# One attention-and-experts kernel on one core: q's and k's transposes as two products of 64 rows each, in one block

## The chip, the core and the metric

The kernel runs on one core of a Trainium2 chip. A core has five engines with queues of their own: TensorE (PE; its weight loads are listed apart as PEld), VectorE (DVE), ScalarE (ACT), GpSimd (POOL) and SyncE (SP), which issues most DMAs. Each works through its own instructions in order and waits on semaphores for the others. The metric is the device time of one execution in microseconds.

## What is computed

The reference has three stages. The first is a linear attention with complex decay over 4 batches, 8 heads, 768 positions and 48 channels; the other two are a gated product and a layer of 8 experts on the 3072 tokens that come out of it.

```
for t in range(S):                       # per batch and head
    new_re = ar * S_re - ai * S_im       # a_re, a_im of step t, scaled to a length of at most 0.999
    new_im = ar * S_im + ai * S_re
    kv = outer(k[t], v[t])
    S_re, S_im = new_re + kv, new_im
    y[t] = q[t] @ S_re
x = y as [3072, 384]
x = (x @ w_a * (x @ w_b)) @ w_out        # 384 -> 1536 -> 384
out = x + gate * (relu(x @ w1[e]) @ w2[e])   # for tokens that a score lets through, e their best expert
```

Everything is float32.

## The kernel before

**Attention in units.** The recurrence is done in chunks of 128 positions. A unit is one chunk of one batch with all 8 heads; there are 24, four for each of six chunks, and two units make a pair. For a unit, ACT and DVE work out the running logarithm and the phase of the decay, with cumulative sums on PE ("l", "tp"), and from them the rotated and scaled q and k: tiles "qr" and "kr", 128 positions by 8 heads by 96 numbers (a cosine and a sine part of 48 each).

`att_pe` (from line 389) is a unit's work on PE. It turns each head of qr and kr to 96 x 128, four heads in one PSUM bank ("pq", "pk", lines 422 and 427), and a copy takes each bank to SBUF ("tq", "tk", line 272, on ACT but for three in the first units). From these come the scores k.q. Units 0 to 5 take whole 128 x 128 products ("pc"). Units 6 to 23 take only the part below the diagonal, in strips of 32 columns of the array, into two banks kept for the purpose ("pcs", line 444); DVE masks them ("sc", line 453). "ds" (line 403) is the update of the running state, "y" (line 482) the output: 32 products in strips, half with the state and half with the masked scores. ACT and DVE take y to the tile "xt", and DVE adds ds to the state. Through units 6 to 19 these three groups stand together: 32 products of pcs, 24 of ds, 32 of y; units 20 to 23 have no ds.

PSUM has eight banks: two with the tag "at", which l, tp, pq, pk, ds, y and the routing's small products share in turn, two "at2" (from unit 6 on the two score banks), two "ab" and two "op".

**The gated product runs alongside.** Every pair gives a group of 256 tokens, 12 groups in all. A group has 12 steps of 18 products in split float32 (a high and a low part, so three products for one), "ab" (lines 615 to 617), whose two halves are multiplied on DVE ("asb", line 623) and split again ("gh", "gl"), and 6 products "op" (lines 599 to 601) for the step two back. While PE works on one group's ab and op, the attention of the next pair is threaded between them. Group 6, for example, runs while units 14 and 15 are made. After the last group the experts follow ("eh", "eo").

**What sets the order.** A scheduler places each engine's instructions by its own model of their times, under the kernel's data dependencies. For the first units a list of names in the code (`ORDER`, applied by `keep_rows`) sets the order by hand. Dependencies added by `after(later, earlier, how)` bind further: with `NoSync` they fix the order alone, with `Sync` they are waited for on the chip.

Of the kernel before, what the change touches and what calls it, by code (L numbers as in the profile page):

```python
# [10 lines left out]
F32 = mybir.dt.float32  # L11
# [5 lines left out]
ALU = mybir.AluOpType  # L17
# [62 lines left out]
GF = 5  # L80
WO = DM + 10
# [37 lines left out]
def kern(tc, q, k, v, a_re, a_im, w_a, w_b, w_out, w_skip, w_gate, w1, w2, out):  # L119
# [3 lines left out]
    with st:  # L123
# [213 lines left out]
        def att_trig(i):  # L337
            c, b = units[i]
            d = U[i]
            im = d["im"]  # L340
            t3 = ew.tile([P, W], F32, tag="t3", name=f"t3_{i}")
            t4 = ew.tile([P, W], F32, tag="t4", name=f"t4_{i}")
            tact(out=t4, in_=im, func=AF.Arctan)
            if c > 0:

                cr = ew.tile([1, W], F32, tag="cr", name=f"cr{i}", bufs=1)
                sync.dma_start(cr, carry[b])
                dve.scalar_tensor_tensor(out=t4[:1], in0=cr, scalar=-2.0 * math.pi, in1=t4[:1], op0=ALU.mult, op1=ALU.add)
            tp = at(f"tp_{i}")
            if i < SPL:  # L350
                pe.matmul(tp[:, :W], trit, t4, start=True, stop=True)
            else:
                hi, lo = parts(i, "t", ("t2", "t1"))
                act.activation(out=hi, in_=t4, func=AF.Copy, scale=INV2PI)
                dve.scalar_tensor_tensor(out=lo, in0=t4, scalar=INV2PI, in1=hi, op0=ALU.mult, op1=ALU.subtract)
                cumsum(tp, hi, lo)

            if on("magic", i) is act:
                act.activation(out=t3, in_=tp[:, :W], func=AF.Identity, bias=b_magic)
            else:  # L360
                dve.tensor_scalar(out=t3, in0=tp[:, :W], scalar1=MAGIC, scalar2=None, op0=ALU.add)
            dve.scalar_tensor_tensor(out=t3, in0=t3, scalar=MAGIC, in1=tp[:, :W], op0=ALU.subtract, op1=ALU.subtract)
            if c + 1 < NCH:
                carry[b] = dpool.tile([1, W], F32, name=f"carry{i}")
                sync.dma_start(carry[b], t3[127:128])
            if on("abs", i) is act:
                tact(out=t4, in_=t3, func=AF.Abs)
            else:
                dve.tensor_scalar(out=t4.bitcast(I32), in0=t3.bitcast(I32), scalar1=0x7FFFFFFF, scalar2=None, op0=ALU.bitwise_and)
            tact(out=t4, in_=t4, func=AF.Sin, scale=-TWO_PI_IN, bias=b_hpi)  # L370
            ts = ew.tile([P, W], F32, tag="t1", name=f"ts{i}")
            d["ts"] = ts
            marks["ts", i] = tact(out=ts, in_=t3, func=AF.Sin, scale=-TWO_PI_IN)
            for nm in ("q", "k"):
                tag = "krl" if nm == "k" and i >= 6 and i % 2 else nm + "r"
                r = ew.tile([P, 2 * W], F32, tag=tag, name=f"{nm}r{i}", bufs=1)
                if nm == "k":
                    d["kf"] = r
                r = r.rearrange("t (h x d) -> t h x d", x=2, d=D)
                src = d[nm].rearrange("t (h d) -> t h d", d=D)  # L380
                on(nm + "c", i).tensor_tensor(out=r[:, :, 0], in0=src, in1=t4.rearrange("t (h d) -> t h d", d=D), op=ALU.mult)
                e = on(nm + "s", i)
                ins = e.tensor_tensor(out=r[:, :, 1], in0=src, in1=ts.rearrange("t (h d) -> t h d", d=D), op=ALU.mult)
                if e is dve:
                    mark((nm + "r", i), ins)
                d[nm + "r"] = r
# [3 lines left out]
        def att_pe(i):  # L390
# [3 lines left out]
            sc, qT = [], []  # L394
# [14 lines left out]
            def new_state(ds):  # L409
                s3 = stt.rearrange("p (h e) -> p h e", e=VP)[:, :, :D]  # L410
                d3 = ds[:96, :W].rearrange("p (h e) -> p h e", e=D)
                if c > 0:
                    dve.tensor_tensor(out=s3, in0=s3, in1=d3, op=ALU.add)
                    d3 = s3
# [7 lines left out]
            def turned(hh):  # L422
                pq = at(f"pq{i}_{hh}")
                for j in range(4):
                    pe.transpose(pq[:96, j * P : (j + 1) * P], qr[:, 4 * hh + j].rearrange("t x d -> t (x d)"), ident)  # L425
                tq = ew.tile([96, 512], F32, tag="tq", name=f"tq{i}_{hh}", bufs=2)
                mark(("tq", i, hh), copy(on("tq", 2 * i + hh, act), tq, pq[:96]))
                pk = at(f"pk{i}_{hh}")
                for j in range(4):
                    pe.transpose(pk[:96, j * P : (j + 1) * P], kr[:, 4 * hh + j].rearrange("t x d -> t (x d)"), ident)  # L430
                tk = ew.tile([96, 512], F32, tag="tk", name=f"tk{i}_{hh}", bufs=2)
                done = mark(("tk", i, hh), copy(on("tk", 2 * i + hh, act), tk, pk[:96])).ins
                qT.append(tq)
                return tq, tk, done

            def scores(hh, tq, tk, done, last):
                pc = at(f"pc{i}_{hh}") if i < CAUSAL else env.pc[hh]
                for j in range(4):
                    if i < CAUSAL:
                        last = pe.matmul(pc[:, j * P : (j + 1) * P], tk[:, j * P : (j + 1) * P], tq[:, j * P : (j + 1) * P], start=True, stop=True).ins  # L440
                        continue
                    for x in (0, 1, 2, 3) if j % 2 == 0 else (3, 2, 1, 0):
                        y0, p0 = j * P + STRIP * (x if j % 2 == 0 else 3 - x), STRIP * x
                        ins = pe.matmul(pc[p0 : p0 + STRIP, y0 : (j + 1) * P], tk[:, y0 : y0 + STRIP], tq[:, y0 : (j + 1) * P], start=True, stop=True).ins  # L444
# [13 lines left out]
            halves = []  # L458
            for hh in range(2):
                halves.append(turned(hh))  # L460
                if i < CAUSAL:
                    last, msk = scores(hh, *halves[hh], last)
            if i >= CAUSAL:
                for hh in range(2):
                    last, msk = scores(hh, *halves[hh][:2], halves[1][2], last)
# [12 lines left out]
            for s_, inter, h, col, begin, end in (t for row in zip(*strips) for t in row):  # L478
                p0, hh, j = STRIP * (s_ % 4), h // 4, h % 4
                o = y[p0 : p0 + STRIP, s_ // 4 * P : (s_ // 4 + 1) * P]  # L480
                l, r = (stt, qT[hh][:, j * P : (j + 1) * P]) if inter else (vt, sc[hh][:, j])
# [12 lines left out]
            dve.tensor_tensor(out=xt[:, :, 1, us], in0=y3, in1=xt[:, :, 0, us], op=ALU.subtract)  # L494
# [734 lines left out]
```

## Time and profile before

| | us |
|---|---|
| runs shown: median (lowest to highest) | 845.05 (844.81 to 845.98) |
| the profiled execution: its time | 847.09 |
| its span, from the first to the last instruction | 845.4 |
| PE busy in the span | 799.0 |
| DVE busy | 559.8 |
| ACT busy | 459.7 |
| mean granted clock of PE | 0.997 |

The span is what the trace covers; the profiled execution's time has some 1.7 us around it. A matmul's record lasts from its start until its result is written, and the records of neighbours overlap, so the cost of a product in a stream is the step from one start to the next and not the length of its record. Several equal records in a row are merged to one line with xN. A shape such as `128*96 128x128` is the weights' rows and columns, and the result's rows and columns as they stream. "idle" before an instruction is time in which its engine did nothing, with the engine and line that ended it; "issue" stands where the profile shows nothing that was waited for.

### The profile page before, as it was taken

What the parts mean: (1) busy time and instruction counts of PE and PEld (TensorE: products, weight loads), DVE (VectorE), ACT (ScalarE), POOL (GpSimd) and SP (SyncE); (2) the same over time, 40 slices, a digit from 0 to 9 for tenths busy, and PEclk for the clock granted to TensorE, in tenths of its full rate; (3) what the DMA queues carried; (4) which work ended last, traced back from release to release, by engine and by line L of the source; (5) the groups of instructions that cost most, each with busy time, mean ns of one, the idle gap of its engine ahead of it and who ended that gap; (6) DMA issues with size and microseconds to landing.
All of it is one profiled execution on the core that took longest, in us unless ns stands there. A gap on an engine that the chain in (4) does not pass through costs nothing.

```text
span 845.4 us, 21833 instructions
## 1 busy us (share of the span) xinstructions
PE 799.0 (95%) x8827; PEld 768.4 (91%) x8827; DVE 559.8 (66%) x1339; ACT 459.7 (54%) x949; POOL 235.0 (28%) x274
## 2 busy tenths in 40 slices
PE   1899999999999999999999999999999999999995
PEld 0589899999999999999999999999999989999995
DVE  7899888695884867738677386673736547555541
ACT  6798655364564655636547365473634325555540
POOL 3131353320311113102130031300304125757650
PEclk9999999999999999999999999999999999999998
DMA  9995223152341522313222132111103239776600
GB/s 256 243 299 131 52 58 77 22 126 38 83 90 25 114 53 72 63 26 85 45 72 58 30 84 45 50 38 28 32 2 115 74 118 347 222 223 199 194 22 23
DMA packets 180959, 83.15 MB, mean 98 GB/s; under 512 B 152084, under 2 KB 168026, under 8 KB 180848
## 3 DMA queue, kind: packets, MB, share of 16 engines
q1 hardware_dynamic: 178800, 76.26, 35.2%
q0 software_dynamic: 2048, 5.40, 1.8%
q8 instruction: 71, 1.16, 0.6%
q14 instruction: 40, 0.33, 0.1%
HBM read 69.84 MB, written 12.61 MB: 98 GB/s over the span
## 4 chain that ended last, share of the span: by engine, by line
PE 80%; DVE 10%; issue 4%; ACT 3%; POOL 1%; DMA 1%; POOLq 0%; ACTq 0%; DVEq 0%
PE ab L615 10%; PE ab L616 10%; PE ab L617 10%; PE op L600 5%; PE op L601 5%; PE op L599 5%; PE y L482 4%; PE eh L901 3%; PE eh L902 3%; PE eh L904 3%; PE eo L918 3%; PE eo L919 3%; PE eo L920 3%; PE pcs L444 2%; PE pq L425 2%
## 5 line engine op out<-in xcount | busy, mean ns | idle before, releaser
L615 PE MATMUL ab<-xt,wa 128*128 128x256 f32 x432 | 124.5, 289 | 7.5 <-DVE asb L623 7.3
L615 PE MATMUL ab<-xt,wb 128*128 128x256 f32 x432 | 123.3, 285 | 0.1
L616 PE MATMUL ab<-xt,wb 128*128 128x256 f32 x432 | 122.8, 284 | 0.0
L617 PE MATMUL ab<-xt,wa 128*128 128x256 f32 x432 | 122.5, 284 | 0.0
L616 PE MATMUL ab<-xt,wa 128*128 128x256 f32 x432 | 122.4, 283 | 0.0
L617 PE MATMUL ab<-xt,wb 128*128 128x256 f32 x432 | 122.2, 283 | 0.0
L623 DVE TENSOR_TENSOR asb<-ab,asb 128x256 f32<-128x256 f32 x144 | 60.3, 419 | 73.0 <-ACT asb L272 71.8
L600 PE MATMUL op<-wo,gh 128*128 128x394 f32 x288 | 99.7, 346 | 1.7 <-POOL wo L512 1.7
L601 PE MATMUL op<-wo,gh 128*128 128x394 f32 x288 | 99.6, 346 | 0.0
L599 PE MATMUL op<-wo,gl 128*128 128x394 f32 x288 | 98.6, 346 | 0.0
L272 ACT ACTIVATE asb<-ab 128x256 f32<-128x256 f32 x139 | 53.0, 381 | 70.1 <-PE ab L617 64.1
L615 PEld LDWEIGHTS ab<-xt,wa 128*128 128x128 f32 x432 | 81.3, 189 | 9.9 <-DVE asb L623 9.1
L272 ACT ACTIVATE gh<-asb 128x256 fp32r<-128x256 f32 x132 | 54.7, 415 | 61.2 <-DVE asb L623 61.2
L616 PEld LDWEIGHTS ab<-xt,wb 128*128 128x128 f32 x432 | 81.4, 188 | 1.3 <-issue 1.2
L617 PEld LDWEIGHTS ab<-xt,wb 128*128 128x128 f32 x432 | 81.3, 188 | 1.1 <-issue 1.0
L615 PEld LDWEIGHTS ab<-xt,wb 128*128 128x128 f32 x432 | 81.4, 188 | 0.9 <-issue 0.6
L616 PEld LDWEIGHTS ab<-xt,wa 128*128 128x128 f32 x432 | 81.4, 189 | 0.7 <-issue 0.4
L617 PEld LDWEIGHTS ab<-xt,wa 128*128 128x128 f32 x432 | 81.3, 188 | 0.0
L627 DVE TENSOR_TENSOR gl<-asb,gh 128x256 fp32r<-128x256 f32 x131 | 60.7, 465 | 30.9 <-ACT gh L272 30.2
L869 POOL TENSOR_TENSOR wq<-stg,wq 128x768 fp32r<-128x768 f32 x32 | 59.5, 1862 | 49.1 <-issue 24.8
L320 POOL TENSOR_TENSOR ll<-t,lh 128x384 fp32r<-128x384 f32 x19 | 19.9, 1050 | 163.1 <-ACT lh L272 118.0
L908 DVE SCALAR_TENSOR_TENSOR hl<-eh,hh 128x256 fp32r<-128x256 f32 x64 | 27.1, 424 | 52.2 <-ACT hh L907 52.1
(257 smaller groups left out, 2123.2 us busy)
## 6 DMA issues: line engine op xcount, KB each, us to landing
stg<-in_moe_w_dram SPq DMA_DIRECT2D x28, 768.0 KB
rawa<-in_moe_w_a_dram SPq DMA_DIRECT2D x6, 768.0 KB
re<-in_a_re_dram SPq DMA_DIRECT2D x24, 192.0 KB
rawb<-in_moe_w_b_dram SPq DMA_DIRECT2D x6, 768.0 KB
q<-in_q_dram SPq DMA_DIRECT2D x24, 192.0 KB
k<-in_k_dram SPq DMA_DIRECT2D x24, 192.0 KB
rawo<-in_moe_w_out_dram SPq DMA_DIRECT2D x6, 768.0 KB
xd<-xr SPq DMA_DIRECT2D x24, 192.0 KB
```

The source lines that it names most:

```text
L272: return act.activation(out=out, in_=in_, func=AF.Copy) if e is act else e.tensor_copy(out, in_)
L482: ins = pe.matmul(o, l[:, col : col + STRIP], r, start=begin, stop=end).ins
L599: pe.matmul(o, gl[:, ts], wh, start=f == 0, stop=False)
L600: pe.matmul(o, gh[:, ts], wl, start=False, stop=False)
L601: i = pe.matmul(o, gh[:, ts], wh, start=False, stop=f == NF - 1)
L615: pe.matmul(o, wl, xt[:, c, 0], start=c == 0, stop=False)
L616: pe.matmul(o, wh, xt[:, c, 1], start=False, stop=False)
L617: pe.matmul(o, wh, xt[:, c, 0], start=False, stop=c == NCC - 1)
L623: dve.tensor_tensor(out=asb, in0=ab[:, 256:], in1=asb, op=ALU.mult)
L627: on("gl", n).tensor_tensor(out=gl, in0=asb, in1=gh, op=ALU.subtract)
L869: lo.tensor_tensor(out=o[:, 1], in0=t, in1=o[:, 0], op=ALU.subtract)
L908: vm = dve.scalar_tensor_tensor(out=gl, in0=o, scalar=0.0, in1=gh, op0=ALU.max, op1=ALU.subtract)
```

## The change

For units 6 to 23 `turned` is replaced by `turned_rows`. Instead of one product for a head, which has 128 rows of weights and streams 128 columns of the identity, there are two: positions 64 to 127 and positions 0 to 63, each with 64 rows of weights and 64 columns of the identity. The two halves write two banks, 64 columns of each for each head, so that one bank holds the upper half of all eight heads and the other the lower half. All of q's 16 products come first (into two "at" banks), then all of k's 16 (into the two score banks, before the scores are written there). A chain of `NoSync` dependencies keeps the 32 in this order; the first of them waits for everything that any of them needs. Four copies on ACT follow, two for q and two for k, each writing 8 heads x 64 columns into the one tile "tq" or "tk" of the unit, 96 x 1024, which now have one buffer each instead of two halves with two. Scores and outputs read the same numbers as before from the new places. Units 0 to 5 keep their whole transposes; only their tiles' names change.

```
+ROWS = 64
...
+            tq, tk = (ew.tile([96, H * P], F32, tag=nm, name=f"{nm}{i}", bufs=1) for nm in ("tq", "tk"))
...
-                    pe.transpose(pq[:96, j * P : (j + 1) * P], qr[:, 4 * hh + j].rearrange("t x d -> t (x d)"), ident)
-                tq = ew.tile([96, 512], F32, tag="tq", name=f"tq{i}_{hh}", bufs=2)
-                mark(("tq", i, hh), copy(on("tq", 2 * i + hh, act), tq, pq[:96]))
...
+            def turned_rows(nm, dst, r, banks, last):
+                for h in range(H):
+                    for x, p_ in ((1, banks[1]), (0, banks[0])):
+                        rows = slice(ROWS * x, ROWS * (x + 1))
+                        ins = pe.transpose(p_[:96, h * ROWS : (h + 1) * ROWS], r[rows, h].rearrange("t x d -> t (x d)"), ident[rows, rows]).ins
+                        for w in [last] if last else [d["krw"], marks["t3", i + 1]] if i % 2 == 0 else [d["krw"]] + env.free:
+                            after(ins, w, mybir.DependencyClass.NoSync if last else mybir.DependencyClass.Sync)
+                        last = ins
+                d3 = dst.rearrange("e (h t) -> e h t", t=P)
+                for x, p_ in enumerate(banks):
+                    cp = copy(act if x == 0 else act, d3[:, :, ROWS * x : ROWS * (x + 1)], p_[:96].rearrange("e (h t) -> e h t", t=ROWS))
+                return last, cp.ins
...
-            if i >= CAUSAL:
                 for hh in range(2):
-                    last, msk = scores(hh, *halves[hh][:2], halves[1][2], last)
+                    turned("q", tq, qr, hh)
+                    turned("k", tk, kr, hh)
+                    last, msk = scores(hh, None, last)
+            else:
+                last, _ = turned_rows("q", tq, qr, [at(f"pq{i}_{x}") for x in range(2)], None)
+                _, done = turned_rows("k", tk, kr, env.pc, last)
+                last = None
+                for hh in range(2):
+                    last, msk = scores(hh, done, last)
```

`d["krw"]` is the instruction that writes the second part of kr, `marks["t3", i + 1]` the one that last reads the phase's bank of the pair's other unit, and `env.free` holds the last readers of the previous unit's y and ds banks.

The scheduler then places everything anew. In the orders below a name's first number is the unit (or, for ab, the group and the step), the last a running one.

PE, group 6, around the first transposes of unit 15, before: four of q, five ab products, four of k.

```order
L616 MATMUL ab6_9_6340<-xt6_5085,wa4_1129 128x256
L425 MATMUL pq15_0_5936<-ident_66,qr15_5799 96x128 x4
L617 MATMUL ab6_9_6340<-xt6_5085,wa4_1129 128x256
L615 MATMUL ab6_9_6340<-xt6_5085,wa4_1129 128x256
L616 MATMUL ab6_9_6340<-xt6_5085,wa4_1129 128x256
L617 MATMUL ab6_9_6340<-xt6_5085,wa4_1129 128x256
L615 MATMUL ab6_9_6340<-xt6_5085,wb4_1191 128x256
L430 MATMUL pk15_0_5943<-ident_66,kr15_5802 96x128 x4
```

And in the changed program the start of the same unit's block.

```order
L630 MATMUL ab6_8_6416<-xt6_5157,wb4_1183 128x256
L628 MATMUL ab6_8_6416<-xt6_5157,wb4_1183 128x256
L629 MATMUL ab6_8_6416<-xt6_5157,wb4_1183 128x256
L436 MATMUL pq15_1_6035<-ident_66,qr15_5883 96x64
L436 MATMUL pq15_0_6034<-ident_66,qr15_5883 96x64
L436 MATMUL pq15_1_6035<-ident_66,qr15_5883 96x64
L436 MATMUL pq15_0_6034<-ident_66,qr15_5883 96x64
```

The pieces of four among ab products have become one run of 32 products, which alternate between two banks.

PE, group 6, inside the output y of unit 14, before: y runs on from the products with the first masked half (sc14_0) to the second (sc14_1).

```order
L482 MATMUL y14_5896<-tq14_1_5826,state2_104 32x128 x2
L482 MATMUL y14_5896<-tq14_0_5812,state2_104 32x128
L482 MATMUL y14_5896<-sc14_0_5851,v14_4885 32x128
L482 MATMUL y14_5896<-sc14_1_5869,v14_4885 32x128
L482 MATMUL y14_5896<-tq14_1_5826,state2_104 32x128
L482 MATMUL y14_5896<-sc14_0_5851,v14_4885 32x128
```

And in the changed program at the same place.

```order
L495 MATMUL y14_5992<-tq14_5891,state2_104 32x128 x3
L495 MATMUL y14_5992<-sc14_0_5947,v14_4945 32x128
L628 MATMUL ab6_7_6384<-xt6_5157,wa3_1042 128x256
L629 MATMUL ab6_7_6384<-xt6_5157,wa3_1042 128x256
L630 MATMUL ab6_7_6384<-xt6_5157,wa3_1042 128x256
L628 MATMUL ab6_7_6384<-xt6_5157,wa3_1042 128x256
L629 MATMUL ab6_7_6384<-xt6_5157,wa3_1042 128x256
L630 MATMUL ab6_7_6384<-xt6_5157,wa3_1042 128x256
L628 MATMUL ab6_7_6384<-xt6_5157,wa3_1042 128x256
L495 MATMUL y14_5992<-sc14_1_5965,v14_4945 32x128
```

Seven ab products now stand between y's first 14 products and the other 18.

ACT, the copies of unit 14's transposes, before: they stand among activations for unit 16 (t1, t2) and the copies of group 6.

```order
L272 ACTIVATE tq14_0_5812<-pq14_0_5807 96x512
L223 ACTIVATE t1_16_6459<-t1_16_6459,b_tiny_80 128x384
L272 ACTIVATE asb6_5_6237<-ab6_5_6212 128x256
L272 ACTIVATE tk14_0_5819<-pk14_0_5814 96x512
L223 ACTIVATE t2_16_6460<-t1_16_6459,b_eps_78 128x384
L272 ACTIVATE gh6_5_6240<-asb6_5_6237 128x256
```

And in the changed program.

```order
L273 ACTIVATE tq14_5891<-pq14_1_5894 96x8x64
L273 ACTIVATE tq14_5891<-pq14_0_5893 96x8x64
L224 ACTIVATE t2_16_6568<-t1_16_6567,b_eps_78 128x384
L273 ACTIVATE tk14_5892<-pcs1_2189 96x8x64
L273 ACTIVATE tk14_5892<-pcs0_2188 96x8x64
L273 ACTIVATE asb6_5_6345<-ab6_5_6320 128x256
```

The four copies stand nearly together, and the copy of the ab tile (asb6_5) has moved behind them.

## Rows read from the trace of the kernel before

**Rows 1.** The page, parts 1 and 4: busy time of PE, and the chain.

```profile
PE 799.0 (95%) x8827; PEld 768.4 (91%) x8827; DVE 559.8 (66%) x1339; ACT 459.7 (54%) x949; POOL 235.0 (28%) x274
...
PE 80%; DVE 10%; issue 4%; ACT 3%; POOL 1%; DMA 1%; POOLq 0%; ACTq 0%; DVEq 0%
```

**Rows 2.** Sums by stage: the stretch of units 6 to 23.

```profile
core 0: us, PE busy (x) PEld busy (x) DVE busy (x) ACT busy (x) POOL busy (x), PEclk, DMA share, GB/s
185.00:640.00 455.00, 445.32 (x5764) 431.26 (x5763) 296.54 (x781) 246.56 (x540) 77.28 (x97) 1.00 0.25 54
```

**Rows 3.** Waits of PE in that stretch: total us, times, longest.

```profile
PE ab L615 <- DVE asb L623: 6.6, 7, 1.0
PE y L482 <- issue: 1.9, 3, 0.8
PE y L482 <- DVE sc L453: 0.9, 1, 0.9
```

**Rows 4.** The transposes from 160 to 645 us: count, ns min/median/max, first and last.

```profile
L425 PE MATMUL pq<-ident,qr x144: 270/272/315, 181.0 to 629.5; 128*96 128x128 f32 x144
...
L430 PE MATMUL pk<-ident,kr x144: 270/272/274, 183.6 to 632.9; 128*96 128x128 f32 x144
```

**Rows 5.** Timeline of PE around four transposes: start, length, instruction.

```profile
184.98 0.28 PE L617 MATMUL ab<-xt,wa 128*128 128x256 f32 x1
...
185.21 0.28 PE L616 MATMUL ab<-xt,wa 128*128 128x256 f32 x1
185.34 0.60 PE L425 MATMUL pq<-ident,qr 128*96 128x128 f32 x4
185.69 0.36 PE L617 MATMUL ab<-xt,wa 128*128 128x256 f32 x1
185.89 0.28 PE L615 MATMUL ab<-xt,wa 128*128 128x256 f32 x1
```

**Rows 6.** Timeline of PE: three records of "pc", unit 5.

```profile
150.94 0.50 PE L440 MATMUL pc<-tq,tk 96*128 96x128 f32 x3
```

**Rows 7.** Timeline of PE: unit 22's y, from the ab before.

```profile
622.84 0.28 PE L616 MATMUL ab<-xt,wb 128*128 128x256 f32 x1
623.04 0.43 PE L482 MATMUL y<-tq,state 96*32 96x128 f32 x8
...
624.94 0.64 PE L425 MATMUL pq<-ident,qr 128*96 128x128 f32 x4
...
625.54 0.28 PE L615 MATMUL ab<-xt,wb 128*128 128x256 f32 x1
```

**Rows 8.** Timeline of PE: pcs, ds and y of unit 14, the ab around them.

```profile
408.52 0.28 PE L615 MATMUL ab<-xt,wa 128*128 128x256 f32 x1
...
412.63 0.28 PE L617 MATMUL ab<-xt,wa 128*128 128x256 f32 x1
```

**Rows 9.** The same of unit 12, with one ab within y.

```profile
354.08 0.28 PE L617 MATMUL ab<-xt,wa 128*128 128x256 f32 x1
...
357.09 0.39 PE L615 MATMUL ab<-xt,wb 128*128 128x256 f32 x1
...
358.85 0.28 PE L617 MATMUL ab<-xt,wb 128*128 128x256 f32 x1
```

**Rows 10.** The copies of q's transposes on ACT, 160 to 645 us; tk alike.

```profile
L272 ACT ACTIVATE tq<-pq x36: 574/594/596, 182.5 to 629.9; 96x512 f32<-96x512 f32 x36
```

**Rows 11.** Timeline of weight loads, unit 21: window ending 575.12, then 575.16.

```profile
575.11 0.12 PEld L425 LDWEIGHTS pq<-ident,qr 128*96 128x96 f32 x1 [0.20 <-issue]
...
575.11 0.17 PEld L425 LDWEIGHTS pq<-ident,qr 128*96 128x96 f32 x2 [0.20 <-issue]
```

**Rows 12.** Timeline of PE: six records of "wt".

```profile
45.21 0.84 PE L561 MATMUL wt<-wg,wtt 128*128 128x10 f32 x6 [0.19 <-ACT wtt L272]
```

**Rows 13.** Timeline of weight loads of "ds", unit 6.

```profile
194.39 0.17 PEld L403 LDWEIGHTS ds<-v,kr 128*32 128x32 f32 x6
194.48 0.16 PEld L403 LDWEIGHTS ds<-u,kr 128*32 128x32 f32 x6
```

More of the change, by code (lines that the diff above doesn't have):

```diff
@@ L361, in att_trig @@
                 dve.tensor_scalar(out=t3, in0=tp[:, :W], scalar1=MAGIC, scalar2=None, op0=ALU.add)
-            dve.scalar_tensor_tensor(out=t3, in0=t3, scalar=MAGIC, in1=tp[:, :W], op0=ALU.subtract, op1=ALU.subtract)
+            marks["t3", i] = dve.scalar_tensor_tensor(out=t3, in0=t3, scalar=MAGIC, in1=tp[:, :W], op0=ALU.subtract, op1=ALU.subtract).ins
             if c + 1 < NCH:
@@ L383, in att_trig @@
                 ins = e.tensor_tensor(out=r[:, :, 1], in0=src, in1=ts.rearrange("t (h d) -> t h d", d=D), op=ALU.mult)
+                d[nm + "rw"] = ins.ins
                 if e is dve:
@@ L393, in att_pe @@
             qr, kr, vt, ee = d["qr"], d["kr"], d["v"], d["ee"]
-            sc, qT = [], []
+            sc = []
             stt = state[b]
@@ L412, in new_state @@
                 if c > 0:
-                    dve.tensor_tensor(out=s3, in0=s3, in1=d3, op=ALU.add)
+                    env.free.append(dve.tensor_tensor(out=s3, in0=s3, in1=d3, op=ALU.add).ins)
                     d3 = s3
@@ L420, in att_pe, with turned @@
             last = None
-            def turned(hh):
-                pq = at(f"pq{i}_{hh}")
+            tq, tk = (ew.tile([96, H * P], F32, tag=nm, name=f"{nm}{i}", bufs=1) for nm in ("tq", "tk"))
+            def turned(nm, dst, r, hh):
+                p_ = at(f"p{nm}{i}_{hh}")
                 for j in range(4):
-                    pe.transpose(pq[:96, j * P : (j + 1) * P], qr[:, 4 * hh + j].rearrange("t x d -> t (x d)"), ident)
-                tq = ew.tile([96, 512], F32, tag="tq", name=f"tq{i}_{hh}", bufs=2)
-                mark(("tq", i, hh), copy(on("tq", 2 * i + hh, act), tq, pq[:96]))
[L428 to L434, printed above, removed]
@@ L436, in scores @@
-            def scores(hh, tq, tk, done, last):
+                    pe.transpose(p_[:96, j * P : (j + 1) * P], r[:, 4 * hh + j].rearrange("t x d -> t (x d)"), ident)
+                mark(("t" + nm, i, hh), copy(on("t" + nm, 2 * i + hh, act), dst[:, 4 * P * hh : 4 * P * (hh + 1)], p_[:96]))
+            def turned_rows(nm, dst, r, banks, last):
[10 more added lines that the diff above has]
+                return last, cp.ins
@@ L437, in scores @@
+            def scores(hh, done, last):
                 pc = at(f"pc{i}_{hh}") if i < CAUSAL else env.pc[hh]
                 for j in range(4):
+                    tks, tqs = (x[:, (4 * hh + j) * P : (4 * hh + j + 1) * P] for x in (tk, tq))
                     if i < CAUSAL:
-                        last = pe.matmul(pc[:, j * P : (j + 1) * P], tk[:, j * P : (j + 1) * P], tq[:, j * P : (j + 1) * P], start=True, stop=True).ins
+                        last = pe.matmul(pc[:, j * P : (j + 1) * P], tks, tqs, start=True, stop=True).ins
@@ L441, in scores @@
                         continue
                     for x in (0, 1, 2, 3) if j % 2 == 0 else (3, 2, 1, 0):
-                        y0, p0 = j * P + STRIP * (x if j % 2 == 0 else 3 - x), STRIP * x
-                        ins = pe.matmul(pc[p0 : p0 + STRIP, y0 : (j + 1) * P], tk[:, y0 : y0 + STRIP], tq[:, y0 : (j + 1) * P], start=True, stop=True).ins
+                        y0, p0 = STRIP * (x if j % 2 == 0 else 3 - x), STRIP * x
+                        ins = pe.matmul(pc[p0 : p0 + STRIP, j * P + y0 : (j + 1) * P], tks[:, y0 : y0 + STRIP], tqs[:, y0:], start=True, stop=True).ins
@@ L456, in scores @@
                 return last, msk
[L458 to L462, printed above, removed]
-            if i >= CAUSAL:
-                for hh in range(2):
-                    last, msk = scores(hh, *halves[hh][:2], halves[1][2], last)
+            if i < CAUSAL:
+                for hh in range(2):
+                    turned("q", tq, qr, hh)
[7 more added lines that the diff above has]
+                    last, msk = scores(hh, done, last)
             pcs = last
@@ L480, in att_pe @@
                 o = y[p0 : p0 + STRIP, s_ // 4 * P : (s_ // 4 + 1) * P]
-                l, r = (stt, qT[hh][:, j * P : (j + 1) * P]) if inter else (vt, sc[hh][:, j])
+                l, r = (stt, tq[:, h * P : (h + 1) * P]) if inter else (vt, sc[hh][:, j])
                 ins = pe.matmul(o, l[:, col : col + STRIP], r, start=begin, stop=end).ins
@@ L493, in att_pe @@
             act.activation(out=xt[:, :, 0, us], in_=y3, func=AF.Copy)
-            dve.tensor_tensor(out=xt[:, :, 1, us], in0=y3, in1=xt[:, :, 0, us], op=ALU.subtract)
+            env.free = [dve.tensor_tensor(out=xt[:, :, 1, us], in0=y3, in1=xt[:, :, 0, us], op=ALU.subtract).ins]
             if c + 1 < NCH:
```

4 rows, old and new, of the table ORDER are left out of this document.

## The prediction

> **What bounds the kernel now.** I read the page first. TensorE (PE) is busy for 799.0 of 845.4 us, and it is 80% of the chain that ended last; VectorE (DVE) is 10% [rows 1]. Then the sums by stage: from 185 to 640 us, where units 6 to 23 run, PE is busy for 445.3 of 455.0 us at the full granted clock [rows 2]. What is missing there is told by the view of waits: seven waits of about 1 us at a group's start, where an "ab" product waits for DVE to empty a bank (6.6 us), one wait of 0.9 us of "y" for the mask "sc", and three of 1.9 us in all at "y" that the view puts down to "issue", that is, to nothing it can see [rows 3]. So in this stage a microsecond that PE saves ends the kernel a microsecond sooner, unless a new wait takes it. ScalarE (ACT), which copies the transposed tiles out, is busy for 246.6 of these 455 us [rows 2].
>
> **The transposes as they are.** Each unit has 8 of q and 8 of k: 144 records on each of two lines over 18 units, one record for each [rows 4]. Four of them stand between two ab products, recorded as x4 in 0.60 us where one takes 0.27; so they follow each other every 0.11 us [rows 5]. What four cost is read from the ab products around them: from the last one before (185.21) to the second one after (185.89) is 0.68 us; two steps of an undisturbed ab stream (184.98 to 185.21, 0.12 each) take 0.24. The difference, 0.44, is four times 0.11: nothing is lost in going from ab to a transpose and back. A unit pays 16 x 0.11 = 1.75 us, all on the engine that bounds.
>
> **The new block.** It has 32 products instead of 16, each of half the rows and half the columns. If time goes with columns that stream, one takes 0.055 us; if the two row halves work side by side, the 32 take 16 x 0.055 = 0.88 us. The trace of before has no product of 64 rows, so side-by-side work is judged by the nearest thing: "y" places its products in four strips of 32 columns of the array. A unit's y has 32 products of 128 columns, and each is recorded twice, 64 records; "pc", the same number of columns in the full array, steps every (0.50-0.28)/2 = 0.11 us [rows 6]; 64 of them in a row would take 7.0 us. The y of 623.04 is over, and the next transpose begins, at 624.94: 1.90 us [rows 7]. So four strips do work side by side, and I take two row halves to do the same.
>
> Going in and out of the strips costs something that the transposes now don't pay. In rows 7, from the ab product before (622.84) to the second one after (625.54) is 2.70 us; less 0.24 for two ab steps, 0.44 for the four transposes in between and 64 x 0.11/4 = 1.76 for y leaves 0.26. A second estimate: one unit in before has its y interrupted by a single ab product, another does not. Without interruption, 408.52 to 412.63 less two ab steps is 3.87 us [rows 8]; with it, 354.08 to 358.85 less three steps is 4.41 [rows 9]. One more way out and back is 0.54. For the block I take the middle, 0.40; its ends are 0 (as for the transposes of rows 5) and 0.54.
>
> TensorEngine Tiling in the Trainium skill (Key Properties) says that a change of tiling mode, not merely of the tile, drains the engine; the 0.26 and 0.54 agree for strips, and no run here shows it for halves. Without such a drain the block would save 0.87 a unit instead of 0.47.
>
> So: 0.88 + 0.40 = 1.28 instead of 1.75, a saving of 0.47 us a unit, **8.5 us** over 18 units (ends: with 0.54, 0.33 x 18 = 5.9; with 0, 0.87 x 18 = 15.7).
>
> **What the new order adds.** The order on PE shows y interrupted more often: in before only two units have it; in the changed program seven even units have it, three of them twice, ten in all. Eight more interruptions at 0.54 are **4.3 us** back. Were they cheaper, as 0.26, it would be 2.1. What they could win is the wait that they fill: of the four waits at y (2.8 us, rows 3) the 0.9 for the mask is before y's fifth product, where most of the new pauses don't stand; the other three have no cause shown. A pause gives whatever is late there 1 or 2 us, so I count a third of the 2.8, **0.9 us**, won; the ends are 0 and 2.8.
>
> **What costs nothing, and its cover.** The copies on ACT stay 72 of 0.59 us [rows 10], two for q and two for k, but now back to back. Between the block's end and the scores PE has at least 27 ab and op products, over 3 us; q's copies begin when half the block is done, and all four, with one other activation between them, are done 0.6 + 4 x 0.59 + 0.6 = 3.6 us after the block began, 2.3 after it ended. If ACT ran late by more than 1 us, scores would wait, at 18 places. Four ACT instructions in a row hold back the copy of the ab tile queued behind them; its bank is wanted again only a whole ab tile and six op products later (3.2 us at the earliest, and in most units after the scores), so nothing waits. The block's own added waits (k's rotated tile and the phase of the pair's next unit, or the y and state of the unit before) are for work that DVE now has queued ahead of the ab tile whose turn comes 2 to 3 us before the block; behind a late one stands all of PE. I count none and keep 2 us for it. k now goes to the banks of the scores, last read by the masks of the unit before, over 3 us earlier. The seven waits at group starts stay: DVE has the same routing work before the same tile, in a slightly other order; 1 us either way.
>
> **Sum** against the profiled execution (span 845.4, its time 847.09, the median of the runs 845.05): -8.5 + 4.3 - 0.9 = -5.1 us. The profiled execution is 2.0 above the median and the change is far from its start and end, so I take the same difference from the median: 845.05 - 5.1 = 839.95, **840.0 us**.
>
> **Rivals.** *Loads one after another (slower).* Each product needs its own load of 96 columns. Two loads that found the queue empty ended 0.05 us apart: 0.12 from the start for the first, 0.17 for both [rows 11]; at 0.045 each, 32 in a row take 1.44, and with 0.40 the block takes 1.84, 0.09 more than now. Then +1.6 + 4.3 - 0.9 = +5.0, 850.1 us. The change loses from a block of 1.75 - (4.3 - 0.9)/18 = 1.56 on, a pair of loads of (1.56 - 0.40)/16 = 0.072 us. For it: nothing shows two row halves loading at once. Against it: a load of 128 columns alone sets the pace of "wt", whose products have ten columns: (0.84-0.26)/5 = 0.116 each [rows 12]; by that, 32 columns would take 0.029 one after another, but the strips of "ds" load six in 0.09, that is 0.015 each [rows 13]. So tiles load at least two at a time. Chance 0.17.
>
> TensorE: Matmul & The Clock Gate in the Trainium skill (LDWEIGHTS) gives a load as its columns over 1.2, 80 ns for 96 of them whatever the rows; in a queue of one that would be 2.56 us a block, +21.8 us, 866. Rows 11 show about 50 for this kind, so the page's figure is not used, though its rule that rows don't shorten a load is what this rival lives on.
>
> *The halves don't work side by side at all (slower).* 32 x 0.055 + 0.40 = 2.16, +0.41 a unit, +7.4 + 4.3 - 0.9 = +10.8: 856. Rows 7 speak against it. Chance 0.06.
>
> *No price for the mode, waits filled (much faster).* -15.7 + 2.1 - 2.8 = -16.4: 828.6; half of the way there, 834. Rows 7 to 9 speak against it. Chance 0.12.
>
> *It saves, but the pauses and a new wait eat it.* The block saves 5.9, pauses cost 4.3, nothing is won, 1.6 is lost in waits: 0, 845. Chance 0.10.
>
> The forecast has 0.55, with its own range 836 to 843. The range of 0.8 runs from 832 to 850.5: it leaves out the far ends of the first and the third rival and the whole of the second. This kernel's runs tell a change from none at about 0.2%, 1.7 us: faster 0.68 (the forecast, the third rival and a little of the last), same 0.08, slower 0.24.
>
> **What would show it.** In the changed profile: the step between pairs in the block (0.055 or 0.06 us a pair means side by side; 0.09 loads in a row; 0.11 no gain); the block from the last ab before to the second after, less two steps, near 1.28; the ways out of y at 0.54 each; the waits on PE between 185 and 640 us still near 9 us, none of them at pq, none at pcs. If the step is 0.055 and the time is not below 843, the pauses or a new wait have eaten it and my 4.3 is too small; if pq waits for DVE, the added waits were not free.

## The result, and the profile after

The changed kernel takes 837.55 us (median of four runs, 836.57 to 838.70), beside it the kernel before 845.32 (844.81 to 845.98): a ratio of 0.9906, 95% interval 0.9893 to 0.9918, 7.8 us less. Forecast were 840.0, 5.1 less. The profiled execution has a span of 837.0 us and a time of 838.70, the slowest of the four; against that of before both are 8.4 us less, and what the start and the clock did in these two executions has a part in that (below).

The page of the changed kernel, busy time of the engines, then the sums of the stage of [rows 2] and the waits of PE in it, as in [rows 3].

```profile
PE 791.7 (95%) x9115; PEld 754.5 (90%) x9115; DVE 552.8 (66%) x1339; ACT 455.6 (54%) x949; POOL 234.1 (28%) x274
```

```profile
185.00:640.00 455.00, 447.00 (x6129) 425.35 (x6128) 294.88 (x788) 245.24 (x543) 81.04 (x101) 1.00 0.26 56
```

```profile
PE y L495 <- DVE sc L463: 6.2, 4, 2.4
PE ab L628 <- DVE asb L636: 1.2, 2, 0.8
PE y L495 <- issue: 0.5, 1, 0.5
```

Two things are to be seen. PE is still what bounds: 447 of 455 us. And the waits have changed places: the seven of 1 us at the groups' starts are two, while y now waits 6.2 us for DVE's masks where it waited 0.9.

The timeline of PE around a block, unit 21 (in place of [rows 5]; start, length, instruction).

```profile
570.31 0.28 PE L628 MATMUL ab<-xt,wb 128*128 128x256 f32 x1
570.51 0.65 PE L436 MATMUL pq<-ident,qr 64*96 64x64 f32 x16
571.00 0.61 PE L436 MATMUL pcs<-ident,kr 64*96 64x64 f32 x16
571.54 0.39 PE L629 MATMUL ab<-xt,wb 128*128 128x256 f32 x1
571.77 0.28 PE L630 MATMUL ab<-xt,wb 128*128 128x256 f32 x1
```

From the ab before to the second one after is 1.46 us; less two ab steps, 1.22. Over the 18 units it is 1.22 to 1.24. Inside, by the trace's nanoseconds, the two halves of a head start 3 to 4 ns apart and the next pair 56 ns later: two halves together take 0.056 us where a whole product took 0.11.

Unit 12, whose y now has two pauses, that is, runs of other products inside it (in place of [rows 9]).

```profile
352.13 0.28 PE L630 MATMUL ab<-xt,wa 128*128 128x256 f32 x1
...
354.49 0.39 PE L628 MATMUL ab<-xt,wb 128*128 128x256 f32 x1
...
355.73 0.39 PE L629 MATMUL ab<-xt,wb 128*128 128x256 f32 x1
...
356.54 0.28 PE L629 MATMUL ab<-xt,wb 128*128 128x256 f32 x1
...
358.20 0.34 PE L612 MATMUL op<-wo,gl 128*128 128x394 f32 x1
```

352.13 to 358.20 holds pcs, ds, y and ten ab steps (0.12 each): 6.07 - 1.18 = 4.9 us for what takes 3.9 in one piece. I measured every stretch of pcs, ds and y of units 6 to 23 in this way, less the idle time within: 71.8 us in 24 stretches before, 76.1 in 32 after. Eight more ways out and back cost 4.3 us, 0.54 each, but 0.6 of it is not theirs. From 246.3 to 249.6 us, in and behind unit 8's y, the granted clock of this execution was 0.50, the lower level of 1.2 GHz:

```profile
246.30:249.60 3.30, 3.30 (x28) 2.92 (x26) 2.76 (x6) 1.35 (x3) 1.22 (x1) 0.50 0.33 63
```

```profile
245.98 0.30 PE L495 MATMUL y<-sc,v 128*32 128x128 f32 x1 [1.97 <-DVE sc L463]
...
247.69 0.41 PE L628 MATMUL ab<-xt,wa 128*128 128x256 f32 x1
247.90 0.41 PE L629 MATMUL ab<-xt,wa 128*128 128x256 f32 x1
```

An ab step took 0.21 us there instead of 0.12, and the stretch of unit 8 before its pause 3.8 us instead of the 3.2 of units 6 and 10. Without that the eight cost 3.7 us, 0.46 each. All 3.4 us at half the rate cost some 1.7 us, an estimate. Before the clock fell PE had waited 1.97 us for a mask; in e2_apart it fell behind a wait of 1.98 us (195.0 to 198.4 us at 0.50), in e12_two_blocks within one of 2.3 us (327.0 to 333.8). The wait of 2.42 us in unit 6 had nothing of the kind behind it. So that the waits cost clock as well is possible, and not shown.

DVE around unit 6's masks ("sc"; "chk" is a reload of unit 0's input for a range test, "re" that of a later unit), and PE's y.

```profile
191.41 0.55 DVE L282 TENSOR_REDUCE immax<-chk 128x1 f32<-128x384 f32 x1 [1.26 <-DMA chk<-in_a_im_dram]
...
192.68 0.68 DVE L463 TENSOR_TENSOR sc<-pcs,keep 128x512 int32<-128x512 int32 x1
```

```profile
193.42 0.30 PE L495 MATMUL y<-sc,v 128*32 128x128 f32 x1 [2.42 <-DVE sc L463]
```

DVE stands still for 1.26 us at a test whose reload has not landed; behind the test come two more operations and then the mask. In before the same test ran at 191.59, after a standstill of 0.32, but unit 6's y began only at 195.1 instead of 190.5: the block gave the scores earlier, and they met a queue that had not been cleared for them.

At a group's start, kernel before: the last product of l on PE, the first asb on DVE, the ab product that waits for it.

```profile
271.44 0.34 PE L265 MATMUL l<-lh,tri_r 128*128 128x384 f32 x1
...
278.22 0.39 PE L615 MATMUL ab<-xt,wa 128*128 128x256 f32 x1 [1.00 <-DVE asb L623]
```

```profile
277.75 0.41 DVE L623 TENSOR_TENSOR asb<-ab,asb 128x256 f32<-128x256 f32 x1
```

The same after.

```profile
271.80 0.33 PE L266 MATMUL l<-lh,tri_r 128*128 128x384 f32 x1
...
278.72 0.39 PE L628 MATMUL ab<-xt,wa 128*128 128x256 f32 x1
```

```profile
278.25 0.42 DVE L636 TENSOR_TENSOR asb<-ab,asb 128x256 f32<-128x256 f32 x1
```

From l to asb it is 6.3 us before and 6.45 after: a chain through ACT and DVE that PE cannot shorten. But after, six more op products (step 10 of the group, 1.07 us) stand behind l instead of ahead of it, so PE has work until asb is done.

**The account of the profiled spans:** blocks 18 x (1.75 - 1.23) = -9.4; more pauses +3.7; the stretch at clock 0.50 some +1.7; waits at y (2.8 to 6.7) +3.9; waits at groups' starts (7.3 to 1.2, unit 22's among them) -6.1; a short wait gone, -0.2; the start -1.2; sum -7.6 of -8.4, so that 0.8 is not accounted for. The start is no work of the change: the warming products, the same in both, ran at nearly half the rate in before's profiled execution.

```profile
L583 PE MATMUL warm<-ts,ident x4: 847/847/1006, 25.1 to 27.1; 128*128 128x384 f32 x4
```

```profile
L596 PE MATMUL warm<-ts,ident x4: 486/486/590, 25.0 to 26.1; 128*128 128x384 f32 x4
```

### The profile page after: what moved, and what is told of

Its sections match the earlier page's. It is cut to its first block, busy times and chain, and to the rows that moved or that the text cites. A ratio compares the mean times of both kernels' runs of the same rounds, so it can differ in the third digit from the quotient of the medians.

```text
span 837.0 us, 22417 instructions
## 1 busy us (share of the span) xinstructions
PE 791.7 (95%) x9115; PEld 754.5 (90%) x9115; DVE 552.8 (66%) x1339; ACT 455.6 (54%) x949; POOL 234.1 (28%) x274
## 4 chain that ended last, share of the span: by engine, by line
PE 78%; DVE 7%; ACT 6%; DMA 4%; issue 3%; POOL 1%; SPq 0%; POOLq 0%; ACTq 0%; DVEq 0%
PE ab L628 11%; PE ab L630 10%; PE ab L629 10%; PE op L613 5%; PE op L614 5%; PE op L612 5%; PE y L495 5%; PE eh L914 3%; PE eh L915 3%; PE eh L917 3%; PE eo L931 3%; PE eo L932 3%; PE eo L933 3%; ACT t L224 2%; PE pcs L454 2%
## 5 line engine op out<-in xcount | busy, mean ns | idle before, releaser
L613 PE MATMUL op<-wo,gh 128*128 128x394 f32 x288 | 99.6, 346 | 1.7 <-POOL wo L525 1.7
L614 PE MATMUL op<-wo,gh 128*128 128x394 f32 x288 | 99.2, 344 | 0.0
L612 PE MATMUL op<-wo,gl 128*128 128x394 f32 x288 | 98.8, 346 | 0.0
L640 DVE TENSOR_TENSOR gl<-asb,gh 128x256 fp32r<-128x256 f32 x131 | 58.9, 450 | 30.4 <-ACT gh L273 29.8
```

Of the source, the lines that this page charges most:

```text
L612: pe.matmul(o, gl[:, ts], wh, start=f == 0, stop=False)
L613: pe.matmul(o, gh[:, ts], wl, start=False, stop=False)
L614: i = pe.matmul(o, gh[:, ts], wh, start=False, stop=f == NF - 1)
L640: on("gl", n).tensor_tensor(out=gl, in0=asb, in1=gh, op=ALU.subtract)
```

## The experiments

Ratios are to runs of the kernel before on the same chip (medians there 846.4 to 846.7 us); 0.0012 is 1 us. The changed kernel has 0.9906.

**Whole transposes in the block (e1_whole).** Edit of the changed kernel:

```
-                    for x, p_ in ((1, banks[1]), (0, banks[0])):
-                        rows = slice(ROWS * x, ROWS * (x + 1))
-                        ins = pe.transpose(p_[:96, h * ROWS : (h + 1) * ROWS], r[rows, h]..., ident[rows, rows]).ins
+                    for p_ in (banks[h // 4],):
+                        ins = pe.transpose(p_[:96, h % 4 * P : (h % 4 + 1) * P], r[:, h]..., ident).ins
...
```

The copies change with it: each takes four whole heads of one bank.

> The changed kernel with one part undone: the 16 transposes of a unit are made of whole 128 rows again (16 products instead of 32, head h into bank h // 4, plain 96x512 copies), still all in one block and with the new order of the work around it. Theory (the two halves of a head run side by side, and that is the gain): a unit's block goes from 1.23 us, changes of tile mode included, to 16 x 0.109 = 1.75 us, +0.52 us for each of 18 units, so +9.4 us: 847 us (845.5 to 848.5), 1.011 times the changed kernel. Rival (the gain is the new order of the work, the fewer waits at the groups' starts, and the halves only pay for their own changes of mode): within 2 us of the changed kernel's 837.6 us.

Measured: 845.95 us, ratio 0.9992 (0.9982 to 1.0003), 7.3 us above the changed kernel. The block is 1.75 us in each unit, 9.4 us more in all; PE's waits are 3.0 us fewer (8.0 to 5.0), which gives 6.4; two more pauses (34 stretches, 77.5 us) make up for most of the rest. So the halves carry the gain; the rest of such an order, pauses included, is worth nothing by itself.

**The halves one after another (e2_apart).** The two loops changed places: eight upper halves, then eight lower ones.

> The changed kernel with the halves not alternated: in each block first the eight heads' second halves, then the eight heads' first halves, so that neighbours in the queue use the same 64 rows. Theory (a pair is cheap because its two halves run beside each other): the 32 products take 32 x 0.055 = 1.76 us and with the way in and out 2.1 us instead of 1.23: +0.88 us x 18 = +16 us, 853.5 us (850 to 856). Rival (a half is cheap by itself, since it has half the rows): block and time stay, 837.6 us within 1.5.

Measured: 843.82 us (840.26 to 845.72), ratio 0.9956 (0.9939 to 0.9973): +4.2, neither the theory's number nor the rival's. PE in unit 21's block:

```profile
575.23 0.28 PE L628 MATMUL ab<-xt,wb 128*128 128x256 f32 x1
575.44 0.75 PE L436 MATMUL pq<-ident,qr 64*96 64x64 f32 x13
575.98 0.26 PE L436 MATMUL pcs<-ident,kr 64*96 64x64 f32 x1
576.03 0.22 PE L436 MATMUL pq<-ident,qr 64*96 64x64 f32 x1
...
576.18 0.71 PE L436 MATMUL pcs<-ident,kr 64*96 64x64 f32 x13
576.82 0.39 PE L629 MATMUL ab<-xt,wb 128*128 128x256 f32 x1
577.05 0.28 PE L630 MATMUL ab<-xt,wb 128*128 128x256 f32 x1
```

The block is 577.05 - 575.23 - 0.24 = 1.58 us, 1.59 on the average of the 18. Within one half the products follow each other every 56 ns, as the theory has it: a half alone is not cheap. But at each change of half the next one's products start while the last three or so of the other half are still to start (k's first at 575.98, between q's). At three borders that hides some 9 of 32 steps, 0.5 us. The block costs 0.36 x 18 = 6.6 us more, fewer waits (8.0 to 6.4) give 1.6 back: +5.0, within the interval. In every run of halves the bank changes with the half, so no run tells the rows from the banks; for whole products a change of bank does nothing, as op steps 0.18 us within a bank (L613 to L614) and into the other one (L614 to L612) alike.

**The range tests behind the masks (e3_tests_late).**

```
-                test(i, t)
+                after(test(i, t).ins, marks["sc", i + 6, 1])
```

> The changed kernel with the range tests of units 0 to 5 (the two DVE operations on reloaded inputs that stand in the queue around units 6 to 11) put behind the masks of the unit they used to stand in front of; the same work is done. Theory (y of units 6, 8 and 10 waits 2.4, 2.0 and 1.6 us because DVE stands still at a test whose reload has not landed, with the mask behind it): these waits go but for a few tenths: -5 us, 832.5 us (831 to 834.5). Rival A (the masks are late from DVE's own work, of which the tests are only 0.55 us each): -1 to -2 us, 836. Rival B (the standstill only moves behind the mask, and the next step's asb waits for it): 837 to 838.

Measured: 833.41 us, ratio 0.9839 (0.9826 to 0.9852), -5.7. PE's waits:

```profile
PE ab L628 <- DVE asb L636: 0.8, 2, 0.5
PE y L495 <- issue: 0.6, 2, 0.3
PE y L495 <- DVE sc L463: 0.6, 3, 0.2
```

The 6.2 us are 0.6. The theory stands: DVE's standstill at the reloads made them, not its own work (the tests' 0.55 us each).

**y without pauses (e7_whole_y).** On top of e3_tests_late, with `late` called for ab of steps 7 and 8 and op of steps 5 and 6:

```
+        def late(g, ins, here):
+            if here and 2 <= g <= 8:
+                after(ins, env.yl[2 * g + 2])      # the last product of that unit's y
```

> The kernel e3_tests_late with y of units 6, 8, 10, 12, 14, 16 and 18 made in one piece: the products that stood in its pauses (up to 12) come behind it. The same work is done. Theory (each pause costs the column products' way out and in again: 0.75 us for a unit with one pause, 0.95 with two): seven units give back 5.5 to 6 us, less new waits of y for its masks of up to 0.3 us each, so 828.5 us (827 to 831) where e3_tests_late is 832.5. Rival (the pauses cost nothing, as their products have to be made anyway, and without them y waits for the masks as long as they lasted, 0.8 us and more each): 1 us faster to 5 us slower than e3_tests_late.

Measured: 835.02 us, ratio 0.9858 (0.9844 to 0.9872), 1.6 slower than e3_tests_late. By the intervals that is at the edge of no difference at all, but far from the theory's 5 faster: the rival holds.

```profile
PE y L496 <- DVE sc L464: 4.6, 13, 0.9
PE y L496 <- issue: 1.0, 2, 0.6
```

Seven units lose their pauses and y waits 4.4 us more (5.6 for 1.2). A pause has its price, but here it filled a wait at least as large. What makes the masks late is in DVE's rows of unit 12, kernel e3_tests_late:

```profile
347.87 0.55 DVE L279 TENSOR_SCALAR_CACHE_REDUCE re<-re 128x384 f32<-128x384 f32 x1 [0.24 <-DMA re<-in_a_re_dram]
...
348.35 0.69 DVE L463 TENSOR_TENSOR sc<-pcs,keep 128x512 int32<-128x512 int32 x1
348.95 0.55 DVE L312 SCALAR_TENSOR_TENSOR t<-t,t 128x384 f32<-128x384 f32 x1
349.42 0.68 DVE L463 TENSOR_TENSOR sc<-pcs,keep 128x512 int32<-128x512 int32 x1
```

In the even units the next pair's test, waiting for its own load, and an operation on t stand ahead of and between the masks.

**The masks first (e8_masks_first).** On top of e3_tests_late, for the test `least` and the operation on t1 of unit i:

```
+            if i >= 8:
+                after(ins.ins, marks["sc", i - 2, 1])
```

> The kernel e3_tests_late with the two DVE operations of unit i (8 and up) that stood between or before the masks of unit i - 2 put behind them: the range test of a_re, which waits for its load, and the operation on t before l. The same work is done. Theory (y waits or is paused in the even units because DVE stands at a test whose load has not landed, with a mask behind it; a pause costs the way out and in): y is whole in every unit and takes 3.88 us as in the odd units, instead of 4.63 (one pause) and 4.8 to 5.2 (two): seven units give 0.75 to 1.2 us each, -6 us against e3_tests_late: 827.5 us where that was 833.4 (825.5 to 829.5). Rival (the postponed test makes l, and with it the next unit's transposes, late by what it spared y): 832 to 835.

Measured: 827.92 us, ratio 0.9780 (0.9768 to 0.9793): 5.0 less than e3_tests_late by the ratios, 10.7 less than the changed kernel, 18.6 less than before. The same work is done, and it is the fastest of all. With the masks early the scheduler left y whole in every unit of its own accord. PE at unit 12, then DVE's masks there:

```profile
341.03 0.28 PE L633 MATMUL ab<-xt,wa 128*128 128x256 f32 x1
341.24 1.33 PE L459 MATMUL pcs<-tq,tk 96*32 96x128 f32 x64
...
345.14 0.28 PE L635 MATMUL ab<-xt,wa 128*128 128x256 f32 x1
```

```profile
342.10 1.29 DVE L468 TENSOR_TENSOR sc<-pcs,keep 128x512 int32<-128x512 int32 x2
```

4.11 less two steps is 3.87 us, the number of [rows 8]. All stretches of pcs, ds and y together are 69.7 us in 22, against 76.0 in 33 in e3_tests_late.

**Only the halves undone there (e11_masks_whole).** The edit of e1_whole in e8_masks_first.

> The kernel e8_masks_first with whole transposes of 128 rows in its blocks (16 products, as in e1_whole): only the halves are undone, where neither pauses nor waits at y can answer. Theory (a block costs 1.23 us with alternated halves, 1.75 whole): +0.52 x 18 = +9.4 us against e8_masks_first (8.4 to 10.4). Rival (part of the halves' gain was only fewer waits): +4 to +7 us, as the step from the changed kernel to e1_whole was +7.3.

Measured: 835.40 us, ratio 0.9871 (0.9856 to 0.9886), +7.5 to +7.7, between the theory and the rival. Its blocks are 1.75 us, again 9.4 in all; PE waits 1.0 us less than in e8_masks_first (2.6 to 1.6), the stretches are 0.6 shorter: 7.8. So the theory's 9.4 is the block's price, and what surrounds it took 1.6 to 2 us of it, in a kernel with hardly a wait to give.

**Step 10's op products behind l, in before (e5_before_op).**

```
+                if i >= 8:
+                    for x in env.op:               # the first op products of step 10, one per bank
+                        after(x, marks["l2"])
```

> The kernel before (whole transposes, four apiece among the others) with one thing of the changed kernel's order added: in the groups with units 8 and up, the six op products of the group's step 10 come behind the next units' l products instead of before them. No work is added or taken away. Theory (the fewer waits of ab for asb at the groups' starts are 6.1 us of the changed kernel's 8.4, and come from this place alone: the chain from l by ACT and DVE to asb takes some 6.2 us in either kernel, and 1.07 us more of PE's work stands behind l): the eight waits of 0.92 to 1.0 us go to under 0.2, so -6 us against before: 0.993 of it, 840.3 us where before is 846.4 (839 to 842). Rival (DVE's order of the routing and asb sets them, so they stay or turn up elsewhere): 845 to 847.5.

Measured: 842.57 us, ratio 0.9954 (0.9940 to 0.9967): -3.9, less than the theory's 6 and more than the rival.

```profile
PE y L485 <- DVE sc L456: 2.8, 4, 1.0
PE ab L620 <- DVE asb L628: 0.7, 2, 0.4
```

The cause of the waits is shown: of 7.3 us of waits for asb 1.4 are left in all (0.7 in this stretch, the rest at unit 22's). The time got only 3.9, as the new order gave y two more pauses: the stretches went from 71.8 to 73.3 us, +1.5.

**The masks first in before (e9_before_masks).** Both edits of e8_masks_first in the kernel before.

> The same two edits as e8_masks_first (late tests of units 0 to 5, masks ahead of the next units' test and t) made in the kernel before, which has whole transposes. Theory: before has only 2.8 us of waits at y and two pauses (1.1 us) to give back: -3.5 us, 843 us where before is 846.4 (841 to 845), so that the changed kernel's advantage grows from 8 us to some 15. Rival (the waits are as large in before, hidden under other names, and it gains as much as the changed kernel, 11 us): 835 us.

Measured: 847.99 us, ratio 1.0013 (1.0002 to 1.0025), a miss: 1.1 slower.

```profile
PE pt L755 <- POOL sl L743: 4.5, 5, 1.0
PE ab L620 <- DVE asb L628: 3.0, 3, 1.4
PE ab L621 <- DVE xt L499: 1.5, 4, 0.7
```

Its waits at y are nearly gone (2.8 to 0.8) and no y is paused (71.8 to 70.0). But in its order the second unit's l and the routing stand among the group's first ab products and no longer ahead of them, and PE waits for POOL's and DVE's part of the routing and for xt: 11.1 us of waits in all where there were 10.4. These sums make -1.1, not +1.1; the 2 us between are not accounted for. So the edits that are worth 10.7 us after the change are worth nothing before it; why the scheduler put l there was not tried.

**Two blocks instead of one (e12_two_blocks).** In e8_masks_first k's first transpose waits for the copy of q's.

> The kernel e8_masks_first with a unit's block of 32 half products cut into two blocks of 16, q's and k's, with 11 to 28 full products between them. No work is added. Theory (each way out of full products and in again costs a block 0.35 to 0.40 us: 1.23 us = 32 x 0.027 + 0.36): 18 more of them, +6.5 us against e8_masks_first (5.5 to 8), 834.4 us where that was 827.9. Rival (the way out and in overlaps with loads that are hidden anyway): within 1.5 us of it.

Measured: 853.32 us, ratio 1.0075 (1.0056 to 1.0093), 25 us above e8_masks_first. The term is right, the total far off. One of its blocks:

```profile
572.42 0.28 PE L635 MATMUL ab<-xt,wa 128*128 128x256 f32 x1
572.63 0.65 PE L441 MATMUL pcs<-ident,kr 64*96 64x64 f32 x16
...
573.43 0.28 PE L634 MATMUL ab<-xt,wa 128*128 128x256 f32 x1
```

573.43 - 572.42 - 0.24 = 0.77 us by these digits, 0.775 to 0.785 in all of them by the trace's nanoseconds. Two are 1.56, one of 32 is 1.23: a way out and in is 0.33, 6.0 us for 18. Another 15 us are new waits (2.6 to 17.8), the largest of them at ab; the stretch at clock 0.50, 6.8 us long, cost its profiled execution up to 3.4 more:

```profile
PE ab L634 <- DVE xt L512: 5.5, 7, 2.3
PE pt L768 <- POOL sl L756: 4.5, 5, 1.0
```

The second block can start only when q's copy is done, and at the chain's end the group's first products wait for xt. By these waits, a chain that had been hidden beside PE no longer was; that it is the copy's 2 us alone was not tried.

## Why the prediction was right, and where it was not

The direction was right, the size 2.7 us short. Two steps failed, by +4.8 and by -6.1 us, and that they nearly cancel is luck: either one alone, added to the 840.0, leads out of the range of 836 to 843.

**The block: right, a little small.** 0.88 + 0.40 = 1.28 was forecast, 1.23 came: the products are 32 x 0.028 = 0.89 and the way out and in is 0.33 (e12_two_blocks), not 0.40. So the term of 8.5 is 9.4. Side-by-side halves, taken over from y's strips, are shown by the pairs' starts and by e2_apart. "TensorE: Matmul & The Clock Gate" in the Trainium skill (The mechanism) describes such tiles as starting some 4 ns apart; the trace has 3 to 4. "TensorEngine Tiling (Array Packing)" in the Trainium skill (Key Properties) says that a change of tiling mode drains the engine; 0.33 us a block agrees.

**The rival of the loads** is out: a pair takes 0.056 us, where 0.072 would have decided. Two loads of 96 columns, one for each half, go into each 0.056 us. "TensorE: Matmul & The Clock Gate" in the Trainium skill (LDWEIGHTS) would have 80 ns for each of them; the trace does not agree. (The forecast's 866 us for that price leaves out its own 4.3 and 0.9; with them it is 870.)

**The pauses: right, a little large.** Eight more at 0.54 were forecast, 4.3 us; measured 4.3, of which 0.6 was the clock: 3.7.

**The waits at y: wrong, and in sign.** The step "I count a third of the 2.8, 0.9 us, won" failed; the waits grew by 3.9. I asked whether a pause would cover the old waits, and not what stood on DVE ahead of the masks at the new, earlier time. The rows were there: a test with a reload pending stood some 4 us ahead of unit 6's masks in before, too. e3_tests_late shows it.

**The groups' starts: wrong.** "The seven waits at group starts stay" failed: -6.1, with unit 22's, instead of 0 within 1. I looked at DVE's routing, whose length indeed did not change, and not at how much of PE's work stands between l and the product that waits; e5_before_op shows that the six op products are enough. These two steps are together -2.2 where I had -0.9.

**What was to cost nothing** did: PE waits at no pq and no pcs in the stage, so the block's first wait and ACT's four copies in a row are free, and the 2 us kept for them were not used. The median fell by 7.8 (6.9 to 9.0 by the interval): by the terms -9.4 + 3.7 + 3.9 - 6.1 - 0.2 = -8.1, without the start and the clock, which differ between executions.

## What to carry to other kernels

A product on half the rows paid in full only beside its twin in the other half (a block of 1.23 us; 1.59 with the halves apart, 1.75 whole), and in one block: each way out and back into full products took 0.33 us alone, about 0.5 in the midst of y. When a change brings work earlier on the engine that bounds, read in the other engines' queues what stands ahead of the operations that answer it, a wait for a DMA above all: moving such tests, and one operation on t, behind the masks gave 10.7 us, more than the change itself, and nothing before the change (e9_before_masks). And a pause that a scheduler puts into a sequence can be a sign that something in it is late, as it was here; take away the lateness, not the pause.

## What was unexpected of the hardware

- By their recorded starts, products for another half of the rows begin ahead of up to about three products that stand before them in the queue (e2_apart: the other half's first at 575.98, the queue's earlier ones at 576.03 and after). So what the opening says of every engine, that it works in order, does not hold for starts on PE. Halves need not alternate one by one for part of the gain: 0.16 of the 0.52 us a unit remain without it.
- The four warming products took 847 ns each in eight of the eleven profiled executions and 486 in three (the changed kernel, e7_whole_y, e5_before_op), with the same code. The trace's record of the granted clock begins, at full, at 24.4 to 24.9 us in these three, ahead of the products, and at 29.3 to 31.2 us, behind them, in the eight. It is a start that differs by 1.2 us without the kernel's doing.
- In the changed kernel's profiled execution the clock fell to 0.50 for 3.4 us in the midst of a stage where PE is busy for 98% of the time, right behind a wait of 2 us.
